# Nine products of a cleared tile on TensorE, ahead of and between the first turns of an attention and feed-forward kernel

## Chip, cores and metric

The kernel runs on one core of a Trainium2 chip. The metric is the device time of one execution in microseconds (us), as the median of several runs. The profile is of one execution of its own, and its span runs from the first to the last instruction of the program.

## What is computed

Eight batches (8 heads, 576 positions, head size 64) go through attention with a relative position bias, and the result through a feed-forward layer with a snake activation. Cut to what matters:

```python
scores = scale * np.matmul(q, k.transpose(0, 1, 3, 2))
scores = scores + bias_table[bucket].transpose(2, 0, 1)[None]
attn = np.exp(scores - max); attn = attn / (sum + 1e-09)
x = np.matmul(attn, v)            # laid out as 4608 tokens x 512
h = x @ w_in                      # 512 -> 2048
s = np.sin(alpha * h)
g = h + s * s / (alpha + 1e-09)
out = g @ w_out                   # 2048 -> 512
```

## The kernel before, in words

The work is a graph of small tasks (`_graph`). Each task has the engines that may run it, the tasks that it waits for and, where it writes to the accumulator `acc`, a bank of eight. The order of the tasks is written out by hand in one long text, `ORDER`: each word names a task, and behind a slash the bank and, with a letter, the engine (`r10/A` is task r10 on ScalarE, `th00/7` is task th00 in bank 7). `_planned` reads it from left to right and emits each task on its engine. An engine runs its own tasks in just that order; between engines only waits on data and on freed buffers count.

The names that are used below, t being the batch and p a pair of heads:

- `r..` loads the first pair of k and q (SyncE's and ScalarE's queues), `f..` casts it to f16 (line 661 on VectorE, 659 on ScalarE).
- `n...`, `v..`, `y..`, `wi.`, `wo.` are loads that GpSimd issues: natural k and q (line 589), v (595, 601), w_in (606) and w_out (611). GpSimd issues them in turn, and later ones wait for earlier ones to land.
- `th..` and `t...` are "turns": transposes of k or q on TensorE (lines 696 and 711), six or twelve small products against an identity. `ch..` and `c...` copy the turned data out of `acc`, mostly on VectorE. The first, second and third turn of TensorE's order are `th00`, `th10` and `th01`.
- `T....` and `X...` are score products (lines 774, 733 for the short tail, 757), `ET`, `EX` their exponentials on ScalarE (787), `BT`, `BX` the multiplication with the bias on VectorE (810, and 796 with the masks `mt`).
- `bu`, `be`, `bs`, `bm`, `bc` make the bias row from the table, `j.` spread it to the tile `toep` by DMA (670), and `m.` copy the masks `mt` from it, on GpSimd (676).
- `A...` and `L.` are the products with v (818, 823, 834), `N` the division by the sums (855, 856).
- `I` is the product with w_in (900), `Z` the sine (906), `Q` the square (911, 913), `G` the activation (918), `O` the product with w_out (928), `W` and `D` the copy out and the store.

At the start TensorE's order is `th00 th10 th01 T0000 T0001 bu th11 t020 t021 bm T0010 ...`. VectorE's is `iz` (clear the identity, line 556), `ms` (twelve memsets, lines 580 to 586, the last of each half being that of a tile `kd`), and then the first cast `f00`. The tiles `kd` hold zeros, into whose diagonal blocks the last columns of k are copied from batch 2 on; `kd[1]` is first used for batch 3.

Of the kernel before, what the change touches and what calls it, by code (L numbers as in the profile page):

```python
# [45 lines left out]
def _graph(K):  # L46
    tasks = {}

    def add(key, engs, emit, deps=(), bank=0, ring=None):
        assert key not in tasks  # L50
        t = tasks[key] = _Task(key, engs, emit, [d for d in deps if d is not None])
        t.bank, t.ring = bank, ring
        return t
# [8 lines left out]
    ms = add("ms", "DVE", lambda e, b: K.memsets())  # L62
# [278 lines left out]
PE_X, KD = 1, 2  # L341
# [3 lines left out]
r10/A r00 iz ms r11/A r01 n011 tab/A sub id cst al n020 n021 n100 f00 n031 f10/A th00/7 th10/6  # L345
n010 f01/A ch00 ch10/A y00 th01/7 T0000/0 ch01 v00 f11 T0001/2 ET0000 bu/7 n131 th11/5 n030 be
ET0001 t020/6 bs ch11 t021/4 n121 c020 bm/7 n111 c021 T0010/0 bc T0210/2 ET0010 j0 j2/G T0201/4
t011/7 ET0210 j1/G t010/6 c011 ET0201 T0211/0 j3 v03 c010 T0200/2 at/7 ET0200 T0101/4 v01 av
t100/6 ET0101 t031/7 c100 y01 t030/3 t131/2 c031 v02 ET0211 T0100/4 c030 n110 ET0100 c131 T0300/0
n101 X00r/6 ET0300 BT0210 BT0200 n231 T0110/2 t111/5 BT0000 n130 ET0110 T0011/0 t121/4 BT0001 c111  # L350
ET0011 n200 X01r/2 BT0010 c121 m0 EX00r X00q/0 BT0201 m1 X01q/4 BT0110 BT0101 EX01r BT0100 T0311/6
wi1 BX00r BT0011 EX01q A000/3 n210 BT0300 n220 EX00q m3 A010/2 N000 ET0311 m2 BT0211 A001/5 N010
n120 n230 t110/4 N001 wi2 t101/3 BX01r c110/A wi0 T0111/0 c101 T0301/6 T0310/4 ET0111 y11 A020/2
A021/3 ET0301 wi3 BT0111 T1000/0 N020 y10 ET0310 S0/7 t130/6 N021 v12 t231/2 ET1000 BT0301 T1001/4
BX00q A011/3 BT0311 v11 ES0 c231 c130/A X10r/0 n221 ET1001 A030/7 BT0310 N011 P00/6 BS0 EX10r
P02/2 A031/3 N030 BX01q T1011/4 Y02/A N031 t220/7 ET1011 T1100/0 Y00 wo0 T1300/2 c220 P01/6 ET1100
P03/5 Y01 t120/4 BT1011 t210/7 ET1300 T1010/0 c120 L0/6 ET1010 Y03 t230/4 NL0 t200/5 v10 T1311/2
c200 T1301/0 I0.8/6 ET1311 v13 c230 ET1301 S1/5 c210 X11r/2 I0.0/4 BT1000 EX11r BT1100 I0.3/7 n211
ES1 Z0.0 BS1 wo1 BT1010 I0.9/5 BT1300 v21 PL0/3 I0.7/2 YL0 Z0.9 wo2 Q0.0 I0.1/3 Z0.3 Q0.9 n201
G0.0 Z0.7 I0.12/1 Q0.3/A G0.9 I0.2/4 Z0.8 G0.3 Q0.7/A I0.5/5 Q0.8 wo3 Z0.2 G0.7 I0.14/7 Z0.1 Q0.2  # L360
g31 Q0.1/A G0.8 I0.10/2 Z0.12 G0.2 I0.13/6 Q0.12/A BX10r G0.1 Z0.10 I0.4/4 g30 BT1001 Z0.14 G0.12
A100/3 Q0.10/A Q0.14 Z0.5 I0.11/1 G0.10 Z0.4 G0.14 y20 I0.6/0 Q0.4/A BX11r g40 Z0.11 N100 I0.15/7
G0.4 Q0.5/A O0.0/3 Z0.6 G0.5 O1.0/2 Q0.6/A O0.2 v22 Z0.15 O0.4 G0.6 T1101/4 Z0.13 O1.2 Q0.11
ET1101 Q0.15 O0.6 G0.11 A101/0 BT1301 O0.8 G0.15 A130/1 N101 O1.4 v20 N130 Y10 O1.6 Q0.13 X11q/4
y21 T1111/0 G0.13 t211/7 ET1111 O1.8 c211 O0.10 EX11q BT1111 T1200/0 O1.10 BT1311 ET1200 t201/7
t221/6 v23 T1110/4 c221 T1201/0 O1.12 ET1110 BT1200 O1.14 ET1201 c201 O0.12 T1310/4 W1 X10q/6
ET1310 T1210/0 BT1101 O0.14 BT1110 BX11q A110/2 BT1201 EX10q W0 A111/5 BT1310 D0 ET1210 N110
A120/4 N111 T1211/6 T2100/2 o2 T2110/0 ET1211 Y11 O3.0/5 BT1210 BX10q O3.2 ET2100 BT1211 O3.4
X20r/6 N120 ET2110 A131/3 S2/4 A121/2 EX20r N131 T2200/0 N121 ES2 O3.6 ET2200 BT2100 T2111/6 Y12
T2101/2 O2.0/4 ET2111 O3.8 X21r/0 ET2101 Y13 O3.10 O3.12 EX21r O3.14 k30 T2000/2 T2201/6 T2211/0  # L370
ET2000 O2.2 O2.4 ET2201 O2.6 O2.8 ET2211 BT2201 O2.10 BT2101 W3 T2001/2 T2210/6 BT2111 T2010/0
ET2001 D3 L1/5 BT2200 ET2010 I1.5/3 BX21r D1 BX20r v33 ET2210 T2310/0 v32 k31 I1.8/2 ET2310 y30
I1.1/7 Z1.5 g71 A210/6 I1.14/1 N210 Z1.8 NL1 I1.15/0 y31 Q1.8/A Q1.5 I1.0/6 Z1.14 G1.5 g50 Z1.1
Q1.14 I1.2/5 G1.8 Z1.0 I1.7/3 Q1.0/A BT2110 G1.14 v30 A220/2 G1.0 Z1.7 I1.13/1 g41 Q1.1/A N220
Z1.2 I1.6/6 G1.1 Q1.7/A Q1.2 I1.4/2 o3/A G1.7 Z1.6 I1.3/7 BT2000 Z1.4 G1.2 O2.12 Z1.15 O2.14 Q1.4
Q1.6/A I1.10/5 G1.4 W2/A Q1.15 g51 O5.0/3 Z1.3 G1.6 I1.12/4 Q1.3/A G1.15 Z1.13 I1.9/6 G1.3 Z1.10
O6.0/2 Q1.13 Z1.12 I1.11/7 G1.13 Z1.9 Q1.10 X21q/0 Q1.9 Z1.11 O5.2 G1.10 g60 EX21q O6.2 Q1.11 O5.4
BT2210 G1.9 A211/5 O5.6 G1.11 O6.4 BT2211 v31 T2011/6 T2300/0 Q1.12 O6.6 ET2300 G1.12 O5.8 N211
O6.8 ET2011 O6.10 BT2010 Y21 BT2300 T2301/0 T2311/4 BT2011 T3110/6 O6.12 ET2311 BT2310 BT2001
O5.10 ET2301 O5.12 O6.14 D2 A200/5 ET3110 BT2301 O5.14 N200 W6/A T3300/0 T3011/6 W5 X20q/4 ET3300  # L380
YL1 A221/2 BS2 BT2311 EX20q O4.0/3 N221 O4.2 BT3300 T3301/0 ET3011 T3000/4 A201/2 BX21q ET3301
A230/7 N201 Y22 A231/6 ET3000 N230 X30r/0 N231 O4.4 EX30r O4.6 BX20q T3001/4 k40 L2/2 ET3001
T3101/0 NL2 v42 T3211/6 T3100/4 ET3101 O4.8 v41 O4.10 ET3100 Y23 O4.12 y41 O7.0/2 ET3211 BT3100
X31q/0 g70 T3111/4 O7.2 ET3111 O7.4 O4.14 Y20 EX31q X30q/4 W4 g61 T3201/6 O7.6 EX30q BT3011 S3/3
O7.8 BT3000 ET3201 O7.10 BT3110 X31r/0 BX30r BX31q ES3 T3200/4 v43 BT3001 EX31r BT3111 T3010/6 YL2
BT3201 v40 ET3010 y40 ET3200 BT3010 BT3301 k41 I2.0/3 A300/1 Z2.0 I2.14/0 N300 BT3101 BT3200
BT3211 I2.5/7 Z2.14 D6 o4 Q2.14 I2.13/6 Q2.0 I2.2/1 A310/5 Z2.2 O7.12 Q2.2/A N310 I2.3/4 Z2.5 G2.0
D4 I2.1/5 Q2.5/A G2.2 Z2.13 G2.14 A311/3 O7.14 G2.5 Z2.1 I2.6/1 Q2.13 Q2.1/A G2.13 Z2.3 I2.7/7 BS3
G2.1 I2.11/6 Z2.7 Q2.3 Z2.6 N311 I2.4/5 G2.3 Q2.7/A A301/3 Q2.6/A W7 I2.15/4 Z2.11 G2.6 D7 Q2.11/A
I2.12/2 G2.7 Z2.15 BX31r I2.9/1 Z2.4 G2.11 Q2.15/A BX30q I2.8/7 N301 Z2.9 Q2.4 Y30 I2.10/6 Q2.9/A  # L390
G2.15 Z2.8 G2.4 O8.0/3 Z2.12 O8.2 D5 G2.9 A330/0 Q2.8/A Z2.10 X40r/4 G2.8 Y31 A320/1 EX40r N330
O8.4 Q2.10 O8.6 N320 O9.0/7 G2.10 O9.2 T3310/0 Q2.12 T3210/4 O9.4 ET3310 G2.12 O10.0/6 ET3210
O10.2 O8.8 T3311/0 BT3210 T4200/4 O8.10 ET3311 A321/2 ET4200 BT3311 O8.12 O10.4 N321 T4300/0
BT3310 T4201/4 Y32 O8.14 ET4300 A331/2 W8 ET4201 L3/1 N331 T4011/4 Y33 NL3 v51 T4010/2 O9.6 ET4011
BX40r O9.8 y50 D8 ET4010 X41r/0 v50 O9.10 T4001/4 EX41r y51 T4211/2 O10.6 v53 ET4001 YL3 O10.8
O10.10 v52 ET4211 T4100/0 T4101/4 O9.12 ET4100 O9.14 O10.12 ET4101 W9 k50 O10.14 BT4200 T4000/0
T4110/2 T4301/4 ET4000 I3.3/7 ET4110 BT4000 S4/1 I3.15/0 BT4001 ES4 W10 ET4301 A400/3 k51 BT4011
I3.1/6 Z3.15 BT4300 I3.6/2 BX41r N400 BT4101 I3.11/1 Z3.6 Q3.15 I3.5/3 Z3.1 G3.15 Q3.6/A I3.0/5
# [595 lines left out]
```

## Time and profile before

| what | value |
|---|---|
| median of 3 runs | 377.55 us (376.06 to 377.68) |
| the profiled execution | 376.66 us |
| its span | 374.6 us |

The span is cut into 40 equal slices of 9.4 us, and the rows of the page that have one digit for each slice show tenths. In the rows in order of time, the first number is the start and the second the time until the last of the group has ended, both in us, and in brackets is how long the engine had stood idle and what ended it. Matmuls are pipelined: of several in a row the starts are closer together than the duration of one. In the rows by stretch, behind the length of the stretch stand busy time and count of PE, its weight loads, DVE, ACT and POOL, then the granted clock, the share of the DMA engines and GB/s.

### The profile page before, as it was taken

The page shows a single profiled execution, that of the slowest core. Times are in us where ns is not written, and L with a number is a line of the kernel's source. Part 1 is how long each engine was busy: PE and PEld are TensorE (multiplying, and loading weights), DVE is VectorE, ACT ScalarE, POOL GpSimd, SP SyncE. Part 2 cuts the span into 40 slices and gives each one's busy share as a digit, 9 for nine tenths or more (in the row PEclk, how much of TensorE's full clock was granted, in tenths as well). Part 3 has the DMA queues.
Part 4 walks back from the last instruction along what each step waited for, and adds up shares of the span by engine and source line. Part 5 has one row for each costly group of instructions (what it writes and reads, how often), then busy time and mean ns, then how long its engine had stood idle before and what let it go on. Part 6 is the DMA issues. An engine that isn't in the chain of part 4 may idle for free.

```text
span 374.6 us, 9138 instructions
## 1 busy us (share of the span) xinstructions
PE 365.4 (98%) x3769; PEld 194.3 (52%) x3769; DVE 267.1 (71%) x615; ACT 310.5 (83%) x416; POOL 86.6 (23%) x105
## 2 busy tenths in 40 slices
PE   4999999999999999999999999999999999999996
PEld 3567445654464555445554555445645554444453
DVE  5799899639975896399747975795739856768402
ACT  5899998999999998999998989999999845686301
POOL 8896682049308100500000050500000000000000
PEclk9999999999999999999999999999999999999999
DMA  9999999999999991970374096960220032020005
GB/s 175 213 165 183 186 197 158 147 209 142 157 149 144 189 138 25 123 117 2 100 154 72 3 106 134 163 31 30 51 78 3 15 87 76 2 84 0 2 36 188
DMA packets 140744, 39.64 MB, mean 106 GB/s; under 512 B 126064, under 2 KB 136160, under 8 KB 140704
## 3 DMA queue, kind: packets, MB, share of 16 engines
q0 software_dynamic: 92864, 18.45, 59.0%
q1 hardware_dynamic: 46224, 18.61, 23.4%
q10 hardware_dynamic: 1616, 2.00, 1.6%
q8 instruction: 29, 0.48, 0.5%
q14 instruction: 11, 0.09, 0.1%
HBM read 36.86 MB, written 15.34 MB: 139 GB/s over the span
## 4 chain that ended last, share of the span: by engine, by line
PE 93%; ACT 4%; DVE 1%; DMA 1%; issue 1%
PE acc L928 34%; PE acc L900 31%; PE acc L774 10%; PE acc L823 8%; PE acc L818 2%; PE acc L711 2%; PE acc L834 2%; PE acc L728 2%; ACT s L906 1%; PE acc L757 1%; ACT ux L787 1%; DMA toep<-in_k_dram 1%; PE acc L733 1%; ACT s L911 1%; DVE kT L661 1%
## 5 line engine op out<-in xcount | busy, mean ns | idle before, releaser
L928 PE MATMUL acc<-w_out,gb 128*128 128x512 f16 (+1 forms) x592 | 144.3, 374 | 0.0
L900 PE MATMUL acc<-xT,w_in 128*128 128x512 f16 x576 | 134.5, 379 | 0.1
L918 DVE SCALAR_TENSOR_TENSOR gb<-s,inv_a,acc 128x512 f16<-128x512 f16 x144 | 103.2, 743 | 7.2 <-ACT s L911 5.6
L906 ACT ACTIVATE s<-acc,alphaT 128x512 f16<-128x512 f32 x144 | 91.8, 682 | 19.6 <-PE acc L900 18.9
L900 PEld LDWEIGHTS <-w_in 128*128 128x128 f16 x576 | 55.0, 98 | 65.7 <-issue 2.5
L787 ACT ACTIVATE ub<-acc 128x1024 f16<-128x1024 f32 x80 | 78.2, 1027 | 10.1 <-PE acc L774 9.6
L928 PEld LDWEIGHTS <-gb 128*128 128x128 f16 x592 | 52.7, 98 | 59.0 <-issue 7.3
L595 POOL DMA_DIRECT2D v<-in_v_dram x32 | 31.4, 1022 | 139.4 <-PE acc L774 77.0
L787 ACT ACTIVATE gb<-acc 128x1024 f16<-128x1024 f32 x48 | 46.6, 1040 | 3.8 <-PE acc L774 3.6
L913 DVE TENSOR_TENSOR s<-s 128x512 f16<-128x512 f16 x83 | 34.1, 420 | 17.5 <-ACT s L906 17.2
L774 PE MATMUL acc<-qT,kT 64*128 64x256 f16 x512 | 43.9, 284 | 0.4 <-DVE kT L661 0.2
L810 DVE TENSOR_TENSOR ub<-ub,toep 128x1024 f16<-128x1024 f16 (+1 forms) x80 | 36.6, 478 | 7.3 <-ACT ub L787 7.1
L911 ACT ACTIVATE s<-s 128x512 f16<-128x512 f16 x61 | 37.9, 629 | 1.1
L661 DVE COPY outs<-acc 128x512 f32<-128x512 f32 (+1 forms) x24 | 16.2, 677 | 26.7 <-PE acc L928 25.5
L823 PE MATMUL acc<-v,ub 128*128 128x65 f16 x640 | 34.4, 193 | 0.0
L787 ACT ACTIVATE ux<-acc 128x1024 f16<-128x1024 f32 x32 | 32.5, 1034 | 1.1 <-PE acc L728 0.9
L774 PEld LDWEIGHTS <-kT 64*128 64x128 f16 x512 | 20.0, 96 | 23.5 <-issue 18.5
L823 PEld LDWEIGHTS <-ub 128*128 128x128 f16 x640 | 30.5, 97 | 3.0 <-issue 0.5
L810 DVE TENSOR_TENSOR gb<-gb,toep 128x1024 f16<-128x1024 f16 (+1 forms) x48 | 23.1, 501 | 11.5 <-ACT gb L787 11.5
L856 DVE TENSOR_TENSOR xp<-acc,rden 128x256 f16<-128x256 f32 x64 | 27.2, 424 | 2.3
L818 PE MATMUL acc<-vt,ux 128*128 128x130 f16 x128 | 28.2, 221 | 0.5 <-ACT ux L787 0.5
L855 DVE RECIPROCAL rden<-acc 128x4 f32<-128x4 f32 x72 | 12.8, 177 | 20.0 <-PE acc L823 13.5
(74 smaller groups left out, 270.1 us busy)
## 6 DMA issues: line engine op xcount, KB each, us to landing
out_dram<-outs SPq DMA_DIRECT2D x30, 256.0 KB, 2.3
v<-in_v_dram POOLq DMA_DIRECT2D x32, 128.0 KB, 6.9
staged_q<-in_q_dram POOLq DMA_DIRECT2D x5, 576.0 KB, 12.4
staged_k<-in_k_dram POOLq DMA_DIRECT2D x5, 576.0 KB, 13.1
w_in<-in_moe_w_in_dram POOLq DMA_DIRECT2D x4, 512.0 KB, 8.6
w_out<-in_moe_w_out_dram POOLq DMA_DIRECT2D x4, 512.0 KB, 10.5
xT<-in_q_dram POOLq DMA_DIRECT2D x11, 144.0 KB, 5.2
xT<-in_k_dram POOLq DMA_DIRECT2D x11, 144.0 KB, 5.0
```

The source lines that it names most:

```text
L595: self.nc.gpsimd.dma_start(out=self.vs[t % 2][:, c, :, 0:D], in_=src)
L774: self.nc.tensor.matmul(out=s[:, o:o + 256], lhsT=self.kT[t % 2][r, p, 128 * c:128 * c + 128], rhs=self.qT[t % 2][r, p, 256 * w:256 * w + ...
L787: self.nc.scalar.activation(out=c["u"], in_=c["s"], func=AF.Exp, scale=0.125)
L810: self.nc.vector.tensor_tensor(out=io, in0=io, in1=m, op=ALU.mult)
L818: nc.tensor.matmul(out=c["av"][:, 130 * j:130 * j + 130], lhsT=cx["u"][:, o:o + 128], rhs=vt[:, p, :], start=True, stop=True, skip_group_c ...
L823: nc.tensor.matmul(out=c["av"][:, 130 * j + 65 * a:130 * j + 65 * a + 65], lhsT=cells[ch // 2]["u"][:, o:o + 128], rhs=vv[:, ch, 2 * p + a ...
L900: self.nc.tensor.matmul(out=c["h"], lhsT=self.w_in[:, j, 128 * f:128 * f + 128], rhs=self.xT[:, j, 512 * b:512 * b + 512], start=(j == 0), ...
L906: self.nc.scalar.activation(out=c["s"], in_=c["h"], func=AF.Sin, scale=self.alphaT[:, f:f + 1])
L911: self.nc.scalar.activation(out=c["s"], in_=c["s"], func=AF.Square)
L913: self.nc.vector.tensor_tensor(out=c["s"], in0=c["s"], in1=c["s"], op=ALU.mult)
L918: self.nc.vector.scalar_tensor_tensor(out=self.g[b][:, f, :], in0=c["s"], scalar=self.inv_a[:, f:f + 1], in1=c["h"], op0=ALU.mult, op1=ALU ...
L928: self.nc.tensor.matmul(out=c["mo"], lhsT=self.g[b][:, f, 128 * (tau % 4):128 * (tau % 4) + 128], rhs=self.w_out[:, f, at], start=(f == 0) ...
```

## The change

A task `mz` clears `kd[1]` as the first instruction of VectorE, and `ms` leaves that tile out. Nine new tasks `F0` to `F8` on TensorE multiply the cleared tile with itself, in bank 5: 128 rows and 128 columns of weights, all of them zero, against 512 columns (`F0` to `F6`) or 384 (`F7`, `F8`) of zeros. Nothing reads the products. They wait for `mz` only.

```diff
-    ms = add("ms", "DVE", lambda e, b: K.memsets())
+    zero = add("mz", "DVE", lambda e, b: K.memset_kd())
+    ms = add("ms", "DVE", lambda e, b: K.memsets(), [zero])
+    for i in range(NFILL):
+        add(f"F{i}", "PE", lambda e, b, i=i: K.fill(b, 4 if i < NFILL - 2 else 3),
+            [zero], bank=1)
...
-PE_X, KD = 1, 2
+PE_X, KD, NFILL = 1, 2, 9
...
-            nc.vector.memset(self.kd[i], 0.0)
+            if not i:
+                nc.vector.memset(self.kd[i], 0.0)
+
+    def memset_kd(self):
+        self.nc.vector.memset(self.kd[1], 0.0)
+
+    def fill(self, bank, chunks):
+
+        z = self.kd[1]
+        self.nc.tensor.matmul(out=self.acc[:, bank, 0:128 * chunks], lhsT=z[:, 0, :],
+                              rhs=z[:, 0:chunks, :].rearrange("p a n -> p (a n)"), start=True, stop=True)
```

The head of `ORDER`, before and after:

```diff
-r10/A r00 iz ms r11/A r01 n011 tab/A sub id cst al n020 n021 n100 f00 n031 f10/A th00/7 th10/6
-n010 f01/A ch00 ch10/A y00 th01/7 T0000/0 ch01 v00 f11
+r10/A r00 mz iz r11/A r01 ms F0/5 n011 tab/A sub F1/5 id cst al F2/5 n020 F3/5 n021 F4/5 n100
+F5/5 f00 F6/5 n031 f10/A F7/5 n010 f01/A th00/7 th10/6 ch00 F8/5 y00 ch10/A th01/7 v00 T0000/0 ch01 f11
```

On TensorE `F0` to `F7` stand ahead of `th00` and `F8` between `th10` and `th01`; on VectorE `mz` stands ahead of `iz`. Elsewhere in the text some forty words change places with neighbours of other engines: read engine by engine, the order of all other tasks is the same as before.

More of the change, by code (lines that the diff above doesn't have):

```diff
@@ L350 @@
[L350 to L367, printed above, removed]
@@ new lines @@
+T0010/0 bc T0210/2 ET0010 j0 j2/G T0201/4 t011/7 ET0210 j1/G t010/6 c011 ET0201 j3 T0211/0 v03
+c010 T0200/2 at/7 ET0200 av T0101/4 v01 t100/6 ET0101 t031/7 c100 y01 t030/3 t131/2 ET0211 c031
+v02 T0100/4 c030 ET0100 n110 c131 T0300/0 n101 X00r/6 ET0300 BT0210 BT0200 n231 T0110/2 t111/5
+BT0000 ET0110 n130 T0011/0 t121/4 BT0001 n200 c111 ET0011 X01r/2 m0 BT0010 c121 EX00r X00q/0 m1
+BT0201 X01q/4 BT0110 BT0101 EX01r wi1 BT0100 T0311/6 BX00r n210 EX01q BT0011 A000/3 n220 BT0300
+EX00q m3 A010/2 N000 ET0311 m2 BT0211 n120 A001/5 N010 n230 t110/4 wi2 N001 t101/3 BX01r wi0
@@ L461 @@
+G8.4 O33.0/6 I7.15/5 I8.11/1 Z7.15 Q7.15/A O30.8 O31.8 Z8.11 G7.15 O31.10 O33.2 Q8.11 O29.12 O28.6
+O30.10 O29.14 O34.0/5 W29 O28.8 G8.11 O28.10 D29 O35.0a/2 O32.2 O34.2 O34.4 O32.4 O34.6 O35.4a
+O34.8 O34.10 O28.12 O33.4 O35.8a O32.6 O30.12 O32.8 O30.14 O34.12 W30/A O33.6 D30/A O32.10 O31.12
+O35.12a O28.14 W35a O31.14 W28 D35a/A O34.14 W31/A O33.8 D28 D31/A O32.12 O33.10 O33.12 W34 O32.14
+D34 O33.14 W32/A O35.0b/7 O35.4b D32 W33 O35.8b O35.12b D33 W35b/A D35b/A
 """
```

202 lines of the change are left out of this document (105 added, 97 removed).

## The prediction

> **What bounds the kernel now.** I read the page first, then the order of time of the first 40 us, then who waited for whom. The page says that TensorE (PE) is busy almost all the time and that its clock was granted in full throughout:
>
> ```profile
> span 374.6 us, 9138 instructions
> PE 365.4 (98%) x3769; PEld 194.3 (52%) x3769; DVE 267.1 (71%) x615; ACT 310.5 (83%) x416; POOL 86.6 (23%) x105
> PEclk9999999999999999999999999999999999999999
> DMA  9999999999999991970374096960220032020005
> ```
>
> The third row can't be taken at its word for the start. The rows of the order of time (start, us, engine, line, what, count) show like work at two speeds:
>
> ```profile
> 4.56 0.69 PE L696 MATMUL acc<-ident,xT 96*64 96x96 f16 x12 [4.56 <-DVE xT L661]
> 5.57 0.45 PE L696 MATMUL acc<-ident,xT 96*64 96x96 f16 x6 [0.32 <-DVE kT L661]
> 11.05 1.17 PE L711 MATMUL acc<-ident,xT 96*64 96x96 f16 x24
> 12.16 1.03 PE L774 MATMUL acc<-qT,kT 64*128 64x256 f16 x8
> 17.29 1.06 PE L733 MATMUL acc<-qT,kT 64*64 64x512 f16 x4
> 20.61 0.90 PE L733 MATMUL acc<-qT,kT 64*64 64x512 f16 x4
> ...
> 24.89 0.70 PE L711 MATMUL acc<-ident,xT 96*64 96x96 f16 x24
> 30.37 0.62 PE L733 MATMUL acc<-qT,kT 64*64 64x512 f16 x4
> 33.36 0.61 PE L774 MATMUL acc<-qT,kT 64*128 64x256 f16 x8
> L733 PE MATMUL acc<-qT,kT 64*64 64x512 f16 x6 | 1.7, 631 | 0.0
> ```
>
> 24 transposes take 1.17 us at 11.05 and 0.70 at 24.89; eight score products 1.03 and 0.61; four of 512 columns 1.06 and 0.62. The four at 20.61 take 0.90, between the two: the clock rose inside them, near 21.2 us. Before that PE ran at about half speed. PE is idle until 4.56, when the first cast (DVE L661) is done. So the change concerns the first 21 us, of which PE works 16.6.
>
> But PE is not alone there. The same stretch on ScalarE, VectorE and GpSimd:
>
> ```profile
> 6.60 1.02 ACT L787 ACTIVATE ub<-acc 128x1024 f16<-128x1024 f32 x1 [0.89 <-PE acc L774]
> 9.54 0.50 ACT L659 ACTIVATE e_sb<-acc 128x392 f16<-128x392 f32 x1 [0.71 <-PE acc L650]
> 18.94 2.19 ACT L787 ACTIVATE ub<-acc 128x1024 f16<-128x1024 f32 x2 [0.41 <-PE acc L774]
> 21.02 3.77 ACT L787 ACTIVATE ux<-acc 128x1024 f16<-128x1024 f32 x4
> 11.86 0.76 DVE L661 COPY qT<-acc 128x576 f16<-128x576 f16 x1 [1.82 <-PE acc L711]
> 19.63 0.76 DVE L661 COPY qT<-acc 128x576 f16<-128x576 f16 x1 [0.66 <-PE acc L711]
> 22.75 0.28 DVE L796 TENSOR_TENSOR ux<-ux,mt 128x256 f16<-128x256 f16 x1
> 26.40 0.28 DVE L796 TENSOR_TENSOR ux<-ux,mt 128x256 f16<-128x256 f16 x1
> 19.61 0.63 POOL L589 DMA_DIRECT2D xT<-in_k_dram  x1 [0.53 <-DMA v<-in_v_dram]
> 20.23 1.65 POOL L676 COPY mt<-toep 64x192 f16<-64x192 f16 x4
> 21.83 0.78 POOL L606 DMA_DIRECT2D w_in<-in_moe_w_in_dram  x1
> 22.60 1.27 POOL L589 DMA_DIRECT2D xT<-in_k_dram  x2
> 23.92 2.06 POOL L676 COPY mt<-toep 64x192 f16<-64x192 f16 x4
> 26.85 0.23 PE L818 MATMUL acc<-vt,ux 128*128 128x130 f16 x1
> PE acc L818 <- ACT ux L787: 0.5, 1, 0.5
> ```
>
> The slow PE makes ACT wait 0.89, 0.71 and 0.41 us and DVE 1.82 and 0.66. From 21 on both run without a break. The last row is the whole list of PE's matmul waits between 21.2 and 53 us: one, of 0.5 us, at 23.01. So from 23 us on PE is the path; what PE does at 26.85 a little earlier ends the kernel as much earlier.
>
> **The change part by part.** *The memset in front.* 0.82 is where DVE's first instruction starts, and clearing one `kd` tile takes 0.27 (rows below), so the products may start at about 0.82 + 0.27 + 0.05 = 1.14 us (0.05 is the step from the cast's end, 3.94 + 0.57, to the first turn at 4.56). The same memset is taken out of the later block, so DVE has nothing more to do, and its next work needs a load:
>
> ```profile
> 0.82 0.11 DVE L556 MEMSET ident<- 128x64 uint32 x1 [0.82 <-PEq L978]
> 1.78 0.27 DVE L586 MEMSET kd<- 128x256 uint32 x1
> 3.94 0.57 DVE L661 CAST xT<-toep 96x384 f16<-96x384 f32 x1 [0.77 <-DMA toep<-in_k_dram]
> ```
>
> Cost nothing: the cast waits 0.77 us for its load, and the identity, cleared 0.27 later than 0.82, is first read at 4.56.
>
> *Eight products ahead of the first turn.* At half speed two pairs of 512 columns take 1.06 us and one product 0.63 from start to end, so one follows the next after 1.06 - 0.63 = 0.43 us. Seven of 512 columns and one of 384 take 7 x 0.43 + 0.32 = 3.3 us and end near 4.5. The first turn starts at 4.56: they fit into PE's idle time. If the first starts late they push the turn by up to 0.2 us; at full speed they would take half. I take 0.
>
> *The ninth product* (384 columns, 0.16 to 0.32 us) goes into the hole of 0.32 us ahead of 5.57. Cost 0 to 0.15; I take 0.
>
> *The clock.* No row of before shows products ahead of 4.56. Half a speed was kept through 16 us of PE work, most of it transposes with products between, and given up inside the densest row of products, at 20.61. Three microseconds of nothing but full-height products are denser than anything before 21 us, so I expect full speed from between 4 and 6.5 us on. [...]
>
> *What a fast PE is worth in the head.* Counted on PE alone: 24 transposes win 0.47, eight score products 0.42, four of 512 columns 0.44. The stretch from 4.5 to 21.2 has 144 transposes, 48 score products and 8 of 512:
>
> ```profile
> L774 PE MATMUL acc<-qT,kT 64*128 64x256 f16 x48 | 6.9, 406 | 0.3 <-DVE kT L661 0.2
> L711 PE MATMUL acc<-ident,xT 96*64 96x96 f16 x120 | 5.9, 281 | 0.0
> ```
>
> That is 6 x 0.47 + 6 x 0.42 + 2 x 0.44 = 6.2 us, the upper bound. Most of it has no taker. GpSimd's queue stands on its loads: its load at 19.61 waited for a v load to land, and the DMA engines are nine tenths busy or more through the first fifteen slices (140 us), so landings don't move when PE does. After it stand four mask copies (L676), three loads, and four more mask copies that end at 23.92 + 2.06 = 25.98. The VectorE multiplication at 26.40 reads these masks, and the attention product at 26.85 reads its result. Today the masks are ready 0.42 us before; afterwards they are what it waits for: 25.98 + 0.05 = 26.03 in place of 26.40, a gain of **0.37 us**. The earlier one at 22.75 waits in the same way for 20.23 + 1.65 = 21.88 and can move by 0.8, which is enough. So everything ahead of 26 us may run up to 2 us early and then stands still. PE has no idle time after that which could win more.
>
> Sum: the profiled execution took 376.66 us, its span 374.6 and 2.06 around it; 376.66 - 0.37 = **376.3 us**. The median of the three runs is 377.55 (376.06 to 377.68), so the profiled one lies 0.9 under it. I take the lower figure as base: a clock that rises some us later in a run, in the dense stretch after 21 us, costs about as much as the runs differ (as worked out in the last rival), and an early rise takes that away. If the spread comes from elsewhere, the same gain gives 377.2.
>
> **The rivals.**
>
> *The masks don't hold it.* Spans on GpSimd are rough, and one of its copies took twice as long as the rest:
>
> ```profile
> L676 POOL COPY mt<-toep x8: 341/350/722, 20.2 to 25.6; 64x192 f16<-64x192 f16 x8
> ```
>
> If all four took 0.35, they would end at 23.92 + 1.4 = 25.3 and give 1.0 us; where they hold nothing, ACT's own waits for PE are the next bound, 0.89 + 0.71 + 0.41 = 2.0. That is 374.7 to 375.6. For it: the waits of ACT and DVE are real and PE is their releaser. Against it: the copies' place behind the loads.
>
> *The change doesn't do what it says.* A product of zeros might not bring up the clock. Then PE does 0.32 us more in a hole of 0.32 and the first turn comes up to 0.2 late: 376.7 to 376.9, or up to 377.8 on the median.
>
> *Slower: up early, down again.* From 6.5 to 21 us ACT's exponentials set the pace, and a PE at twice the speed has half as much to show for it. Two stretches of 3.4 us, with the busy time and count of line 774 alone, of PE and of its weight loads:
>
> ```profile
> 10.99:14.40 3.41, 1.77 (x14) 0.56 (x12) 1.00 1.25 253
> 14.40:17.82 3.42, 1.21 (x8) 0.26 (x8) 1.00 1.80 207
> ```
>
> With some 0.21 us a pair (1.03 us for four pairs, tail included) these score products stream 1.5 and 0.85 us, at full speed 0.75 and 0.43: an eighth to a quarter, the rest transposes and gaps. I found nothing as thin after 21 us, so the trace does not show that the clock survives it. If it falls there and comes back a stretch or two later than today's 21.2, the dense attention work pays: 2.87 us busy of 21.2 to 24.6 and 3.25 of the next 3.4:
>
> ```profile
> 21.20:24.60 3.40, 2.87 (x88) 2.35 (x85) 3.37 (x10) 3.40 (x4) 3.27 (x7) 1.00 0.83 120
> 24.60:28.00 3.40, 3.25 (x82) 2.55 (x79) 3.33 (x10) 3.40 (x6) 3.32 (x7) 1.00 1.25 199
> ```
>
> Of each I take about 2.4 us as streaming (an estimate: busy less the tail of some 0.2 us behind each group of products), so half speed adds 2.4 for one such stretch and 4.9 for two; 376.66 less 0.4 with these is 378.7 to 381.2. It decides when the clock is back after 23 us, where PE becomes the path. [...]
>
> ```profile
> 13.88 2.13 PE L711 MATMUL acc<-ident,xT 96*64 96x96 f16 x48
> ```
>
> **How the numbers follow.** Forecast (0.37 us, 375.7 to 377.2) 0.47; masks don't hold 0.29; no effect 0.13; up and down again 0.11. Likeliest: 376.3 us. The range 374.6 to 378.0 takes in the first three and leaves out the last. Half a per cent, about what a measurement of this kernel can tell from no change, is 1.9 us: under 375.66 is faster, over 379.44 slower. The second case lies under it but for a sliver, with 0.02 of the first: faster 0.30. Of the last, three quarters lie above: slower 0.08. The rest, 0.62, is the same.
>
> **What would show it.** In the profile after: nine products of line `fill` from 1.1 to 4.6 us; the 24 transposes near 11 us in 0.70, not 1.17; no idle of ACT for PE between 10 and 20; the second L796 of DVE right behind the end of GpSimd's second four copies, near 26.0, and its attention product near 26.5; all later rows about 0.4 earlier. Wrong: transposes still at 1.17 (clock not raised), or rows at 0.70 followed by rows at 1.17 before 24 us (fell again), or the second L796 well before 25.9 (masks not the gate).

## The result, and the profile after

| kernel | median | runs | range |
|---|---|---|---|
| before | 376.92 us | 15 | 375.87 to 377.68 |
| after | 377.86 us | 15 | 376.89 to 379.52 |

The ratio of after to before is 1.0027, with a 95% interval of 1.0015 to 1.0039: about 1 us slower where the prediction had 0.37 us faster, and still within the half per cent that it called the same. The profiled execution of after took 379.16 us with a span of 377.0, so it is 1.3 us above its own median, while that of before (376.66) is 0.3 under its own. The two profiles differ by 2.5 us, the medians by 0.9.

The page of after, the rows that answer to those shown of before:

```profile
PE 365.4 (97%) x3778; PEld 193.7 (51%) x3778; DVE 266.2 (71%) x615; ACT 310.5 (82%) x416; POOL 87.4 (23%) x105
PEclk9899999999999999999999999999999999999999
DMA  9999999989999991990364096960130032020005
```

TensorE has as many busy microseconds as before, in a span that is 2.4 us longer: what was lost is waiting. (Of the busy time 3.9 us are now the nine products; all other work is as much shorter.) And the clock row now has one 8, in the second slice. TensorE's rows of after in order of time show the first part of the plan at work:

```profile
1.20 3.49 PE L599 MATMUL acc<-kd 128*128 128x512 f16 x8 [1.20 <-DVE kd L594]
4.61 0.69 PE L710 MATMUL acc<-ident,xT 96*64 96x96 f16 x12
5.24 0.40 PE L599 MATMUL acc<-kd 128*128 128x384 f16 x1
5.62 0.32 PE L710 MATMUL acc<-ident,xT 96*64 96x96 f16 x6
11.04 1.17 PE L725 MATMUL acc<-ident,xT 96*64 96x96 f16 x24
13.65 1.21 PE L725 MATMUL acc<-ident,xT 96*64 96x96 f16 x48
```

The eight products fit into the idle time: the first turn starts at 4.61, in before at 4.56. The six transposes at 5.62 take 0.32 us, not 0.45. But the 24 at 11.04 take 1.17 again, and the 48 at 13.65 take 1.21 (2.13 before). So the clock came up, fell and came up again. The stretches say when (length, busy time and count of PE, weight loads, DVE, ACT, POOL, then the granted clock, DMA share, GB/s):

```profile
1.20:5.41 4.21, 4.21 (x21) 1.64 (x21) 2.44 (x14) 2.39 (x4) 3.99 (x7) 1.00 0.92 203
5.41:8.82 3.41, 2.49 (x43) 1.42 (x44) 1.77 (x6) 2.46 (x4) 2.98 (x5) 1.00 1.26 189
8.82:12.23 3.41, 3.41 (x54) 1.97 (x52) 1.56 (x3) 2.47 (x4) 2.52 (x6) 0.50 1.66 185
12.23:21.20 8.97, 6.51 (x145) 3.84 (x145) 8.43 (x20) 8.97 (x10) 7.79 (x12) 1.00 1.69 207
```

The first row's 1.00 is what the trace puts ahead of its first clock record, which stands at 5.41; the products themselves still follow one another every 0.43 us, where those of 512 columns in I0.8 (39.17) follow every 0.22. After a stretch in which PE was busy 2.49 of 3.41 us came one at 0.50.

By 18 us TensorE is 1.5 us ahead of before. Then three waits eat that and more. The first is at the masks. GpSimd's rows, the copies' durations (min, median, max, then first and last start), and VectorE's rows of after:

```profile
20.18 0.63 POOL L603 DMA_DIRECT2D xT<-in_k_dram  x1 [0.45 <-DMA v<-in_v_dram]
20.81 2.40 POOL L690 COPY mt<-toep 64x192 f16<-64x192 f16 x4
25.24 2.00 POOL L690 COPY mt<-toep 64x192 f16<-64x192 f16 x4
```

```profile
L690 POOL COPY mt<-toep x8: 340/345/1241, 20.8 to 26.9; 64x192 f16<-64x192 f16 x8
  DVE ux L810: 1.7, 2
```

```profile
20.56 1.29 DVE L824 TENSOR_TENSOR ub<-ub,toep 128x256 f16<-128x256 f16 x4
23.23 0.29 DVE L810 TENSOR_TENSOR ux<-ux,mt 128x256 f16<-128x256 f16 x1 [1.39 <-POOL mt L690]
27.27 0.29 DVE L810 TENSOR_TENSOR ux<-ux,mt 128x256 f16<-128x256 f16 x1 [0.29 <-POOL mt L690]
```

VectorE does stand and wait for the masks, twice, 1.7 us in all, as forecast; but the first four are ready at 23.21 and not at 21.88, and the others at 27.24 and not at 25.98. The load ahead of the first four went out 0.57 later than in before (20.18, in before 19.61), and a copy that usually takes 0.35 us took 1.24 while VectorE's four multiplications ran beside it (20.56 to 21.85). It is the first wait, not the second, that reaches A020, the product that started at 26.85 in before. TensorE's rows:

```profile
27.03 0.38 PE L788 MATMUL acc<-qT,kT 64*128 64x256 f16 x3 [0.60 <-DVE xp L870]
27.34 0.23 PE L832 MATMUL acc<-vt,ux 128*128 128x130 f16 x1
```

A020 starts at 27.34, while VectorE's second multiplication with the masks still runs (27.27 to 27.56), so it does not read its result. What TensorE waited for just before, at 27.03, is a division (`xp`), and VectorE's divisions stand behind its first multiplication with the masks. From that one (22.75 in before, 23.23 here) to A020 it is 4.1 us in both kernels. The second wait reaches A021 (0.17 us at 28.28), whose bank is freed by the copy that VectorE makes behind the second multiplication. The other two waits, on TensorE:

```profile
37.62 0.28 PE L788 MATMUL acc<-qT,kT 64*128 64x256 f16 x1
38.64 0.59 PE L788 MATMUL acc<-qT,kT 64*128 64x256 f16 x7 [0.74 <-issue]
123.61 1.04 PE L914 MATMUL acc<-xT,w_in 128*128 128x512 f16 x4 [0.73 <-DMA xT<-xp]
```

The eight score products are those of the tasks T1311 and T1301, four each. At 37.62 the first starts, and the second, of the same task, only 1.02 us later. "issue" is time for which the profile shows nothing that PE waits for: the second product waits on no semaphore. At 123.61 the product I2.0 waits 0.73 us for a transposed x that SyncE's queue brings.

Where the tasks start, in the profiled executions (us; "before again" and "after again" are of the first experiment):

```
                     T0011   A020    I0.8   I0.0    I2.0   last product
before               19.45   26.85   37.34  39.05  121.08  370.68
before again         19.44   26.70   37.20  38.98  120.98  370.55
after                17.91   27.34   39.17  40.81  123.61  373.19
after again          18.60   26.70   38.83  40.48  123.16  372.73
```

Against before, after is 1.54 ahead at T0011, 0.49 behind at A020 (0.83 behind at its sister A021, 28.28 and 27.45), 1.83 behind at I0.8, behind the pause, and 2.53 behind from I2.0 to the end.

### The profile page after: what moved, and what is told of

Read it like the earlier page. It is cut to its first block, busy times and chain, and to the rows that moved or that the text cites. A ratio compares the mean times of both kernels' runs of the same rounds, so it can differ in the third digit from the quotient of the medians.

```text
span 377.0 us, 9156 instructions
## 1 busy us (share of the span) xinstructions
PE 365.4 (97%) x3778; PEld 193.7 (51%) x3778; DVE 266.2 (71%) x615; ACT 310.5 (82%) x416; POOL 87.4 (23%) x105
## 4 chain that ended last, share of the span: by engine, by line
PE 87%; DMA 5%; POOL 3%; ACT 2%; issue 1%; DVE 1%; SPq 0%; POOLq 0%
PE acc L942 33%; PE acc L914 31%; PE acc L788 8%; PE acc L837 8%; PE acc L832 2%; DMA xT<-xp 2%; DMA v<-in_v_dram 2%; DMA xT<-in_k_dram 2%; PE acc L848 2%; ACT s L920 1%; PE acc L742 1%; POOL xT L603 1%; POOL mt L690 1%; PE acc L725 1%; PE acc L771 1%
## 5 line engine op out<-in xcount | busy, mean ns | idle before, releaser
L788 PE MATMUL acc<-qT,kT 64*128 64x256 f16 x512 | 42.0, 275 | 3.0 <-DVE kT L675 1.6
```

The source lines that it names most:

```text
L788: self.nc.tensor.matmul(out=s[:, o:o + 256], lhsT=self.kT[t % 2][r, p, 128 * c:128 * c + 128], rhs=self.qT[t % 2][r, p, 256 * w:256 * w + ...
```

## The experiments

Three theories were at stake. **Masks**: TensorE's early clock lets VectorE run ahead into GpSimd's copies, and stretched copies cost more than the clock gains. **Late loads**: the loads ahead of the copies were late by chance, and the difference is no property of the change. **Position**: the pause at T1311 has nothing to do with clock or masks, but with the number of TensorE instructions ahead of it. A last pair of edits moves the transposition that TensorE waits for at I2.0. In the texts on record the first two also go by the letters M and L. Each ratio is against before on the same chip; the profiles are of single executions, on several chips, and are compared with before again.

### Both kernels again

The kernel before and the kernel after, unchanged, on one chip.

> The kernel before, unchanged: what two executions of one program differ by. Both theories: ratio 1.000 within 0.002. Theory M (the masks on GpSimd come later because VectorE's multiplications, run earlier by the faster TensorE, stretch the mask copies): the clock rises near 21 us, give or take one stretch of 3.4 us, the four first mask copies end near 21.9 us. Theory L (the loads landed later by chance in the one profiled execution of the changed kernel): the second load of k (landed at 7.2 us in the profile of before, 7.9 in that of after) scatters by 0.5 us or more between executions of the same program.

> The changed kernel, unchanged. Theory M: again a first mask copy of over 0.8 us (1.24 in the first profile) and TensorE's products with v behind it; ratio 1.002 to 1.004. Theory L: the copies stay stretched or not by chance, loads land as in before, ratio 1.000 to 1.002. The pause of 1.0 us within one score task at 37.6 us comes back at the same place if it belongs to the program, and not if it is chance.

Before: 377.15 us, ratio 1.0004 (0.9995 to 1.0013). After: 378.16, ratio 1.0037 (1.0023 to 1.0051). The loss is real and of the same size twice. In this profile of after the clock kept full speed from 5.67 to 15.9 us and fell later, the load n020 came at 7.25 us (7.17 in before's profile, 7.95 in after's first), and still the pause stands where it stood:

```profile
38.31 0.59 PE L788 MATMUL acc<-qT,kT 64*128 64x256 f16 x7 [1.04 <-issue]
```

Late loads alone are out, and so are late masks as the whole cause: A020 starts at 26.70, exactly as in before again, so there nothing is lost yet, though the lead of 0.84 us at T0011 is gone. A021 is 0.34 late, I0.8, behind the pause, 1.63, and all from I2.0 on 2.18. In before again the eight run without a break, and the four products of the next task, I0.8, take 1.18 us:

```profile
36.66 0.61 PE L774 MATMUL acc<-qT,kT 64*128 64x256 f16 x8
37.20 1.18 PE L900 MATMUL acc<-xT,w_in 128*128 128x512 f16 x4
```

### The mask copies on VectorE, after and before

```diff
-m0 ... m1 ... m3 ... m2
+m0/D ... m1/D ... m3/D ... m2/D
```

> The changed kernel with the eight mask copies on VectorE, where nothing can stretch them and GpSimd's loads are not behind them. Theory M: the wait for the masks (1.7 us of VectorE's idle time in the profile of after) is gone, and the early clock is worth something: ratio to before 0.995 to 0.999. Theory L, or any cause outside the masks: the ratio stays at 1.002 to 1.004.

> The kernel before with the eight mask copies on VectorE: the control for the run beside it. Theory M: VectorE is saturated from 20.7 us on in before and was not waiting for the masks, so eight more instructions there cost 0 to 0.5 us: ratio 1.000 to 1.0015. If the ratio falls as far as that of the changed kernel with the same edit, the masks' place is worth something by itself, and the products nothing.

After: ratio 1.0103 (1.0077 to 1.0129). The control, before with the same edit: 1.0085 (1.0070 to 1.0101). The copies are short now, 0.20 us, and nobody waits for them, but VectorE's divisions come later and TensorE waits for those instead. The waits are in the control too, so the pair says nothing for or against the masks; the expectation of a gain fell. The pause is there in after and not in before:

```profile
27.41 0.38 PE L788 MATMUL acc<-qT,kT 64*128 64x256 f16 x3 [0.91 <-DVE xp L870]
39.42 0.59 PE L788 MATMUL acc<-qT,kT 64*128 64x256 f16 x7 [1.21 <-issue]
```

### Nine products that do next to nothing, at the head and late

The first kernel cuts each of the nine to 32 weight columns and 8 columns; the second has the same nine behind I0.8.

```diff
-        matmul(out=self.acc[:, bank, 0:128 * chunks], lhsT=z[:, 0, :], rhs=z[:, 0:chunks, :]...)
+        matmul(out=self.acc[0:32, bank, 0:8], lhsT=z[:, 0, 0:32], rhs=z[:, 0, 0:8])
...
-F0/5 ... F8/5 ... T1301/0 I0.8/6 ET1311
+T1301/0 I0.8/6 F0/5 F1/5 F2/5 F3/5 F4/5 F5/5 F6/5 F7/5 F8/5 ET1311     (second kernel only)
```

> The changed kernel with each of its nine products cut to 32 weight columns and 8 columns of the tile: as many instructions for TensorE in the same places, but next to no work. It leaves out no part of the reference. Theory of the position (the pause of about 1 us inside the score task T1311 comes from where the instruction stream is cut into blocks, and eighteen more instructions at the head move that cut into the task): the clock comes up near 21 us as before, and the pause of 1.0 to 1.5 us at T1311 is there all the same; ratio 1.002 to 1.003. Theory of the clock and the masks (the loss follows from the early clock, which makes VectorE collide with GpSimd's copies and brings TensorE early to T1311): without the early clock no pause, task times as before within 0.2 us; ratio 0.999 to 1.001.

> The changed kernel with its nine products cut to 32 weight columns and 8 columns and placed behind the product I0.8, after T1311, near 38 us: eighteen more instructions as in the run with nine tiny ones at the head, but all behind T1311. Position: no pause at T1311, tasks up to it as before the change within 0.2 us; later cuts are moved, so a later pause may come; the nine themselves cost 0.25 to 0.5 us; ratio 1.0005 to 1.0015. Clock and masks: the same, since the clock is as before; ratio 1.000 to 1.001. The run is the control to the nine tiny ones at the head: a higher ratio there is due to the place alone.

At the head: 378.34 us, ratio **1.0036** (1.0024 to 1.0049), as much as the change itself. Late: 377.99, ratio 1.0023 (1.0010 to 1.0037). TensorE's rows of the first:

```profile
1.19 0.38 PE L599 MATMUL acc<-kd 128*32 128x8 f16 x8 [1.19 <-DVE kd L594]
36.83 0.28 PE L788 MATMUL acc<-qT,kT 64*128 64x256 f16 x1
37.76 0.59 PE L788 MATMUL acc<-qT,kT 64*128 64x256 f16 x7 [0.65 <-issue]
122.52 1.04 PE L914 MATMUL acc<-xT,w_in 128*128 128x512 f16 x4 [0.50 <-DMA xT<-xp]
```

and of the second:

```profile
36.94 0.61 PE L786 MATMUL acc<-qT,kT 64*128 64x256 f16 x8
38.45 0.38 PE L597 MATMUL acc<-kd 128*32 128x8 f16 x9
122.55 1.04 PE L912 MATMUL acc<-xT,w_in 128*128 128x512 f16 x4 [1.04 <-DMA xT<-xp]
```

With the nine tiny products at the head the clock comes up at 20.9 us, as late as before (21.2), every task up to 36 us starts within 0.2 us of before, and still T1311 breaks after its first product, for 0.93 us. With the nine behind it, T1311 has no break. So the pause comes from the number of products ahead, and needs neither the early clock nor late masks. The profile of the first ends 1.53 us later than that of the repeated before (378.12, 376.59): 1.0 behind at I0.0, after the pause, and 0.6 more at I2.0. The second loses 0.46 us to the nine products themselves, and 1.1 at I2.0, so its ratio is above what was expected without a pause. The two ratios' intervals overlap, so the times alone do not price the pause; the profiles do.

### Five products

```diff
-PE_X, KD, NFILL = 1, 2, 9
+PE_X, KD, NFILL = 1, 2, 5
-F5/5 ... F6/5 ... F7/5 ... F8/5
```

with all five 512 columns wide. It was run once with timed rounds and, later, twice more for another profile each.

> The changed kernel with five products of 512 columns at the head and none between the second and the third turn (F5 to F8 left out). Position: the cut falls four products, eight instructions, later in the program than in the changed kernel, behind T1311 or inside I0.8; the pause at T1311 is gone or sits elsewhere, and the ratio is 1.001 or less if the early clock remains. Masks: the early clock, if five products suffice for it, still makes the first copies collide; ratio 1.001 to 1.004 as with nine. If five products do not raise the clock early, the run tells only of the position: ratio 1.000 to 1.001 with no pause, 1.002 to 1.003 with one.

> The kernel with five products once more, for another profiled execution. If its time is near its median of 377.6 us, the 1.1 us above the first profile stand at one place: I2.0 near 121 us (0.5 to 1.0 us of idle time of TensorE for xT) by the theory of the late transposition; a longer pause ahead of product 605 (1.0 us or more, not 0.6) by the theory of the position; later masks (A020 0.5 us later than in the first profile) by the theory of the masks.

> The same kernel a third time, with the same three readings; if the three profiles lose at different places, the rest is spread over several waits that come and go.

Timed: 377.62 us, ratio 1.0021 (1.0007 to 1.0034). The three profiled executions took 376.52, 377.66 and 377.84 us, and the clock came up at 13.0, 11.0 and 24.3 us: the same products at the same place, and one time out of three no early clock at all. The last two ran on another chip, where one run of before took 377.54 us. Starts as in the table above:

```
                     T0011   A020    I0.8   I0.0    I2.0   last product
five, first          17.77   26.19   37.27  38.92  120.94  370.54
five, second         17.60   27.04   38.40  40.05  122.07  371.67
five, third          19.43   27.08   38.63  40.27  122.27  371.86
```

The second is the instructive one. It is 1.84 us ahead of the repeated before at T0011, 0.34 behind at A020, 1.2 behind at I0.8, and loses nothing at I2.0. GpSimd's and VectorE's rows of it:

```profile
20.51 0.63 POOL L601 DMA_DIRECT2D xT<-in_k_dram  x1 [1.06 <-DMA v<-in_v_dram]
21.13 1.77 POOL L688 COPY mt<-toep 64x192 f16<-64x192 f16 x4
24.94 2.01 POOL L688 COPY mt<-toep 64x192 f16<-64x192 f16 x4
```

```profile
22.93 0.29 DVE L808 TENSOR_TENSOR ux<-ux,mt 128x256 f16<-128x256 f16 x1 [1.40 <-POOL mt L688]
26.98 0.29 DVE L808 TENSOR_TENSOR ux<-ux,mt 128x256 f16<-128x256 f16 x1 [0.30 <-POOL mt L688]
```

GpSimd waits 1.06 us for a load of v to land, the first four masks end at 22.90, VectorE takes them up at 22.93, A020 follows 4.1 us later, and a lead of 1.8 us is gone. The pause has moved. In the second profile, then the third:

```profile
38.09 0.38 PE L786 MATMUL acc<-qT,kT 64*128 64x256 f16 x3 [0.26 <-issue]
```

```profile
38.32 0.38 PE L786 MATMUL acc<-qT,kT 64*128 64x256 f16 x3 [0.80 <-issue]
```

Now it stands inside T1301: three of the eight products are behind it, not seven. Four products fewer at the head, and it comes four products later in the program. From start to start the gaps are 0.60, 0.53 and 1.06 us.

### Which product it is

Counted in the trace from the start, the product behind the pause is always the one with **605 products ahead of it**, whatever it computes:

| kernel | product number 605 is in | gap ahead of it | from number 477 to 605 |
|---|---|---|---|
| before; again | I0.8 | 0.29; 0.36 us | 5.07; 5.14 us |
| nine late | I0.8 | 0.22 | 4.99 |
| after; again | T1311 | 1.02; 1.32 | 5.46; 5.76 |
| nine tiny at the head | T1311 | 0.93 | 5.36 |
| five (three profiles) | T1301 | 0.60; 0.53; 1.06 | 5.15; 5.08; 5.61 |
| fifty-five tiny (below) | a product with v, line 850 | 0.57 | 6.16 |

In before it is one of I0.8's products, which follow each other every 0.22 us anyway; a gap of 0.29 or 0.36 hides almost all. The page of after counts 3778 products and 3778 weight loads, so 128 products are 256 instructions of TensorE. The page counts fetches of instructions as a DMA queue of their own, in before and in after alike, and one more with fifty-five products at the head:

```profile
q8 instruction: 29, 0.48, 0.5%
```

```profile
q8 instruction: 30, 0.49, 0.5%
```

0.48 MB in 29 pieces are 16 KB each (16384 bytes in the traces of before and after), about one for each 128 of the 3778 products. In the trace such a fetch starts 2.6 to 4.0 us after product 477 in these kernels, while the loads of w_in and v keep the DMA engines full (195 GB/s from 32.78 to 35.45 us of before); it takes 1.0 us, and product 605 starts 1.2 to 1.5 us after its end. DMA queues of the run with nine tiny products, from 32.40 to 35.50 us and then from 35.50 to 36.60 (packets, MB, the time that the packets took as a share of 16 engines' time; it exceeds 100% where packets overlap):

```profile
q0 software_dynamic: 724, 0.59, 125.1%
```

```profile
q0 software_dynamic: 287, 0.20, 123.3%
q8 instruction: 1, 0.02, 5.5%
```

Product 477 started at 32.40 there. For 3.2 us the queues moved data alone, then came the one fetch. Elsewhere the fetch follows sooner, 0.34 us after product 989 in before, at 72.2 us; what makes it late near 33 us was not isolated. That TensorE waits at product 605 for what this fetch brings is the author's reading of the times. One more figure speaks for the fetch. In all nineteen profiles, those without a visible pause too, product 605 starts 1.21 to 1.54 us after the end of the fetch, although the fetch starts anywhere between 2.6 and 4.0 us after product 477; and no product at any other number of the series (every 128 from 93 on) starts less than 1.36 us after the end of its own fetch. Nobody took the fetch away in an experiment, so that the pause stands at product 605 is shown, and that it is the fetch is argued from these times.

### Fifty-five products at the head

If only the time for 128 products counts, other numbers should be better than nine: by the trace of before, the 128 that end nine ahead of its number 605 take 4.4 us, those that end at it 5.1, and those that end fifty-five ahead some 5.5. Three kernels with fifty-five: all tiny, five wide and fifty tiny, four wide and fifty-one tiny. The last was profiled twice.

```diff
-        self.nc.tensor.matmul(...)
+        if i < 5:                          # here and below: 0 in the first kernel, 4 in the third
+            self.nc.tensor.matmul(...)     # 512 columns, as in after
+        for _ in range(50 * (i == 4) + (i >= 5)):
+            self.nc.tensor.matmul(out=self.acc[0:32, bank, 0:8], lhsT=z[:, 0, 0:32], rhs=z[:, 0, 0:8], ...)
```

> Fifty-five products of 32 weight columns and 8 columns at the head and none later: six times as many added instructions as in the run with nine tiny ones, about 1.65 us of TensorE at the 30 ns that one took there, all of it inside TensorE's idle time before the first turn. By the trace of before, 128 products that end nine products ahead of number 605 are done in 4.4 us, and 128 that end fifty-five ahead of it in 5.5 to 5.7 us. Position (product 605 cannot start until a block of instructions is there, about 5.1 to 5.5 us after product 477): no pause of more than 0.3 us ahead of product 605, tasks as before the change within 0.3 us, ratio 0.999 to 1.001. If what costs is the number of added instructions: ratio over 1.004.

> The same with the first five of the fifty-five as wide as in the changed kernel (128 weight columns, 512 columns): the clock should come up near 13 us, as with five products alone. The first turn starts about 0.5 us later, since the products now end near 5 us. Position: no pause ahead of product 605, so that what the early clock brings by 33 us (0.5 us with five products alone, lost again at T1301) stays: ratio 0.0005 to 0.0015 below the run with fifty-five tiny ones. If the gain is lost elsewhere, at the masks or at the transposed x near 121 us, the two ratios agree within 0.0005.

> The same with four wide products and fifty-one tiny ones: they end near 4.5 us, about where the first turn starts without them. If four raise the clock before 14 us, the ratio is that of the run with five or up to 0.001 lower, and it is the version to beat both kernels with; if the clock comes up near 21 us, the ratio is that of the run with fifty-five tiny ones.

> Four wide and fifty-one tiny products once more. Late transposition: idle time for xT near 121 us that the first profile did not have. Position: the pause ahead of product 605 stays 0.5 to 0.7 us and the loss stands elsewhere. Clock: it comes up later than 13 us in this execution, and the tasks before 26 us are as late as in the kernel before.

All tiny: 377.68 us, ratio 1.0014 (1.0001 to 1.0027). Five wide: 378.27, 1.0027 (1.0013 to 1.0040). Four wide: 377.91, 1.0023 (1.0007 to 1.0040). Fifty-five tiny ones cost less than nine (1.0014 and 1.0036, 0.8 us), though the intervals touch: that speaks against the number of instructions as such as the cost, but the clock, which came up early with the fifty-five, differs too. Neither kernel with wide products fell below the tiny ones, as had been expected. And there are pauses all the same, against the expectation. Rows of the first, then of the second (the third has the pause of the first, 0.61 us from start to start):

```profile
1.19 1.63 PE L601 MATMUL acc<-kd 128*32 128x8 f16 x55 [1.19 <-DVE kd L592]
35.12 0.22 PE L850 MATMUL acc<-v,ux 128*64 128x65 f16 x3 [0.38 <-issue]
```

```profile
31.01 0.19 PE L839 MATMUL acc<-v,gb 128*128 128x65 f16 x1 [0.71 <-issue]
37.20 0.23 PE L850 MATMUL acc<-v,ux 128*64 128x65 f16 x3 [0.42 <-issue]
```

From product 477 to 605 took 6.16, 6.19 and 6.19 us, and the fetch started 3.8 to 4.0 us after 477 there; the row at 31.01 is product 477 itself, 128 earlier. The time to the next fetch is no constant (2.67 us after 477 in before), and a place that was safe by before's times was not safe.

The clock surprised here too. With all products tiny it came up at 13.6 us, and with four wide ones at 13.1 and 11.9, with five at 13.3 to fall once more. The best single execution of the study is one of these, the first profile with four wide products (376.09 us, span 373.9), 1.11 us ahead of the repeated before at A020 and 0.5 at the end; its second profile (378.31, on the chip where before took 377.54) was 1.54 us ahead at T0011 and 0.07 behind at A020, VectorE having waited 1.39 us for the first masks again. The range of its runs is 376.09 to 379.12. No version beat before.

### All mask copies ahead of a load

```diff
-n200 ... m0 ... m1 ... m3 ... m2
+m0 m1 m3 m2 n200 ...
```

> The changed kernel with all eight of GpSimd's mask copies ahead of its load n200 instead of four behind that load and four behind the load of w_in. Masks: the multiplications that wait for the mask end earlier, A021 is not later than before the change, and the ratio falls by 0.001 to 0.002 against the changed kernel, to 1.001 to 1.002, with the pause at T1311 still there. Position alone: the shift at T1311 is what it was and the ratio stays near 1.003. If the copies are stretched all the same, they end later than 24.5 us and the run does not decide.

379.21 us, ratio 1.0064 (1.0041 to 1.0087), worse. GpSimd's and TensorE's rows:

```profile
19.78 4.38 POOL L688 COPY mt<-toep 64x192 f16<-64x192 f16 x8
```

```profile
38.99 0.60 PE L786 MATMUL acc<-qT,kT 64*128 64x256 f16 x7 [1.57 <-issue]
```

A020 does start earlier than in before (26.56, repeated before 26.70), but the loads behind the copies are later and the pause is the longest of all, 1.85 us from start to start. And it has a consequence of its own, in the stretches around it:

```profile
35.90:39.44 3.54, 1.97 (x68) 1.57 (x65) 3.50 (x8) 1.17 (x3) 0.86 (x2) 1.00 1.31 204
39.45:42.85 3.40, 3.40 (x20) 0.96 (x18) 1.08 (x2) 2.02 (x3) 1.77 (x2) 0.50 1.83 177
```

The clock falls to half for 3.4 us behind it, in the middle of dense work: I0.8 is 2.3 us late, I0.0 3.6.

### The transposition ahead of I2.0

SyncE's transposition of k for batch 4 (`k40`) moved behind the four small ones of x, in after, in the kernel with four wide products, and, as control, in before.

```diff
-k40 L2/2 ... Y23 ... Y20 ... YL2 BT3201
+L2/2 ... Y23 ... Y20 ... YL2 k40 BT3201
```

> The changed kernel with SyncE's transposition of k for turn 4 (k40) behind YL2 in place of ahead of Y23. If the wait at I2.0 is the rest of the loss: no idle time of TensorE for xT near 121 us, tasks behind I2.0 0.7 us earlier than in the changed kernel, ratio lower by 0.0015 to 0.002, at 1.0010 to 1.0020, and the pause at T1311 as it was. If the wait only moves to another transposition or the executions lose elsewhere: ratio 1.0025 to 1.004 as before.

> Four wide products and fifty-one tiny ones, with k40 behind YL2. Its parent's profiled execution ended 0.5 us ahead of the kernel before, its median 0.9 us behind. If the executions above that profile lose at I2.0: ratio 0.998 to 1.000, spread of the times as small as that of the kernel before. If they lose elsewhere: 1.001 to 1.003 and the same spread.

> Control: the kernel before with k40 behind YL2. Its profile shows no wait of TensorE for xT at I2.0, so the ratio should be 0.999 to 1.0005; a ratio over 1.001 would mean that the moved transposition itself costs something, and that much would have to be taken off the other two.

After: 377.93, ratio 1.0030 (1.0016 to 1.0044). Four wide: 379.57, 1.0089 (1.0066 to 1.0113). Before: 378.18, 1.0036 (1.0023 to 1.0049). In after the wait at I2.0 is gone and nothing comes in its place; its profile is 0.4 us behind the repeated before at T1311, 1.3 behind at I0.8, and 1.2 at the end: what is left of the loss is the pause (0.91 us from start to start) and the time before it. With four wide products the clock came up at 24.1 us this time, and TensorE has gaps, from start to start, of 1.1 us at 128 and 0.8 us at 136 us that the parent's first profile did not have. The control:

```profile
129.26 1.02 PE L898 MATMUL acc<-xT,w_in 128*128 128x512 f16 x4 [1.38 <-DVE xp L854]
```

But in the control a new wait of 1.38 us appears at 129 us, so the edit costs something of its own, and the ratios don't tell what the wait at I2.0 is worth. In before, with no product added at all, the clock came up at 13.2 us in this execution and fell again at 16.6.

## Why the prediction was wrong, point by point

- **The memset and the place of the products: right.** First product at 1.20 (forecast 1.14), first turn at 4.61, 0.05 late, the ninth in its hole.
- **The clock rises early: right, and then the rival's fall.** It came up at 5.4 us, within the forecast 4 to 6.5 (an estimate of the author's: no row of before shows how soon a rise follows dense work), but fell for 3.4 us at 8.8, in the repeat at 15.9. That cost little at that point, since T0011 was still 1.54 and 0.84 us early. "Full speed from between 4 and 6.5 us on" did not hold in any of the five executions with nine wide products: up at 4.0 to 5.7 us in each, down again in each. The rival had the clock back only after 23 us. That did not happen in after, but it did with the masks on VectorE (down from 14.3 to 24.5), and with the transposition moved it was down from 8.6 to 22.2.
- **Cost of the nine products taken as 0: this is the step that failed.** "They fit into PE's idle time" counts them as time of TensorE. They are also eighteen instructions, and with them product 605, ahead of which the pause stands in every kernel, falls nine products earlier in the work, out of I0.8 and into T1311. That a fetch of instructions holds it there is argued from the times above and not shown. Nine tiny ones, which cost no time at the head and leave the clock alone, gave a ratio of 1.0036; the whole change 1.0027 and 1.0037. In the profile the pause is 0.93 us with nine tiny ones, 1.02 and 1.32 after, against 0.29 and 0.36 at the same number in before, where the products are 0.22 us apart anyway. In after again, where nothing is lost at A020, it makes up most of the 1.63 us at I0.8; the rest of the 2.18 at the end comes at I2.0.
- **The masks as the gate: the wrong ones were priced.** VectorE does wait for the masks when TensorE is early, in both profiles of after, in the second with five products and the second with four wide ones. But "the attention product at 26.85 reads its result" is a wrong reading: in after that product starts while the second multiplication with the masks still runs. It hangs on the first one, through VectorE's work behind it, which the prediction let "move by 0.8". And both sums took GpSimd's end as fixed. The first four copies ended at 21.88 and 21.54 in before, at 23.21 and 22.57 in after, at 22.90 in the second with five, because the load ahead of them went out later (20.18 and 20.51, in before 19.61) and because copies were stretched. The gain of 0.37 at that product became a loss of 0.49 in one execution and nothing in the other, and in three executions with other products a gain of 0.5, 1.0 and 1.1. That row moves by more than what was forecast from it.
- **The stretched copy.** The prediction had seen one copy twice as long and let it stand as rough. Some copies run long beside VectorE's multiplications with the bias: of the 136 mask copies that ran on GpSimd in these profiles, 36 took over 0.45 us, and every one of them ended 0.20 or 0.21 us after the end of such a multiplication. The copy of 1.24 us is one, and another of 1.34 us beside the same four multiplications stands ahead of the wait of 1.39 us in the second profile with four wide products. What makes them long is not shown (both read the tile `toep`, and no run takes that away), and the experiment that was to take the copies off GpSimd cost more elsewhere, so the price of the stretch is not measured.
- **"What PE does at 26.85 a little earlier ends the kernel as much earlier": too simple.** Even where TensorE was ahead at A020 (0.5 us with five products, first profile), the pause at product 605 took it back (0.60 us from start to start, I0.8 0.07 behind). Part of a lead can pass: of 1.0 and 1.1 us at A020, with fifty-five tiny and with four wide products, 0.55 and 0.47 were left at I0.8.
- **What stays open.** The ratio of the late nine (1.0023), and how much of the loss of after is at I2.0. That wait (0.4 to 1.2 us) is in both profiles of after, in those of nine tiny, nine late and fifty-five tiny products and of after with the masks on VectorE, and in none of the three with five or of the others with wide and tiny products. It hangs on a queue of SyncE whose transpositions follow one another almost without a gap there (before: 108.7 to 123.8 us), and no run shows its price by itself. Nor does any run show what the early clock alone is worth.

## What to carry over

An instruction that costs no time of its own still has a place in the stream (nine tiny products at the head: ratio 1.0036): before an instruction is called free, count what it shifts, and when a row shows a pause "issue" inside one task, compare the product's number, not its line, between the kernels. A dummy with as many instructions and no work is the control that tells an effect of the work from one of the place. And a gate taken from one profile (a GpSimd queue behind loads) has a spread: with five products the first four masks ended at 21.6, 22.9 and 21.5 us in three executions, a spread more than three times the gain that was forecast. That a row starts behind another does not show that it reads it, either: look in the run after whether it ever starts before the other has ended.

## What the runs showed of the hardware

- The granted clock rose early without any wide product (fifty-five tiny ones: 13.6 us; no product at all: 13.2), and did not with five wide ones in one execution of three (24.3). An early rise in a single profile proves little about its cause. With nine wide ones it came up at 4.0 to 5.7 us in all five executions, and in no other before 11.0; in all five it fell again, for 3.4 to 13.7 us at a time.
- It fell to half after a 3.4 us stretch in which PE was busy 2.49 us, and after one with 1.97, though no row in them shows PE waiting longer than 1.6 us at a time. A stretch of after with 2.1 us (from 22.47 on) kept the clock, so the busy time alone does not tell. With four and five products it held for the rest in four of five profiles that had an early rise.
- TensorE stood 0.5 to 1.85 us, from start to start, inside a task with nothing to wait for in the profile, always at the same number in its own stream (605, and in two executions also 477, which is 128 less). At 605 it starts 1.2 to 1.5 us after the end of a fetch of instructions, in all nineteen profiles.
- Of 136 GpSimd copies, most of them of 0.35 us, 36 took over 0.45 and up to 1.34 us beside a VectorE multiplication of two tiles, and each of the 36 ended 0.20 or 0.21 us after the end of one.
